# Six batches of attention by weighted values and row strips, in an attention and MLP kernel on one Trainium2 core

## The chip, the core and the metric

The kernel runs on one core of a Trainium2 chip. Its engines run side by side, each through its own instructions in order: TensorE (PE, with weight loads shown as PEld), VectorE (DVE), ScalarE (ACT), GpSimd (POOL) and SyncE (SP), which mostly issues DMAs. The metric is the time of one execution on the device in microseconds, lower is better. Before the change it was 351.64 us, the median of three runs.

## The reference

There are 8 batches of 8 heads, 576 positions of 64 numbers. A gate s gives each position a forget sum; the scores get the difference of two sums added, then a causal softmax and the product with v follow. The result, laid out as (8, 576, 512), goes through a layer norm and a two-layer MLP with a residual.

```python
scores = scale * np.matmul(q, k.transpose(0, 1, 3, 2))
cum = np.cumsum(np.maximum(s, 0.0), axis=-1)
bias = -(cum[:, :, :, None] - cum[:, :, None, :])
scores = np.where(causal, -1000000000.0, scores + np.minimum(bias, 0.0))
attn = softmax(scores)                 # row maximum taken off, 1e-09 in the denominator
x = np.matmul(attn, v)                 # heads put side by side: (8, 576, 512)
xn = (x - mu) / np.sqrt(var + 1e-06) * g_ln
out = x + np.maximum(xn @ w_ch1, 0.0) @ w_ch2
```

## The kernel before

*Tiles.* 576 positions are four tiles of 128 and a tail of 64. Scores are computed with keys on the partitions, so that exp of them can be the stationary operand of the product with v. `scores(b, h)` (L320) fills three PSUM banks, `sa`, `sb` and `sc`, with the causal blocks of keys 0 to 511; `scores_d(b, j)` (L358) does the last 64 keys for two heads. ACT takes exp of each bank into `er`, one of four slots; POOL sets the part above the diagonal to zero (L348, L378; the first ten heads add a mask on PE). `pv(b, h)` (L396) multiplies with `v_bf`, in 15 matmuls of 65 columns: the last column of v is one, so that it gives the softmax's denominator. `pv_norm` (L415) divides on DVE: a reciprocal, a product into `xb` for the four tiles, one into `xm` for the tail. The tails of two batches share one `xm` tile.

*Bias.* The difference of the forget sums comes out of the score matmul itself: k and q have 64 rows of numbers and 4 more rows, three bf16 pieces of the sum and ones (`KA` = 68). For the first two groups (four heads are a group) they stand beside the numbers before the transpose; for groups 2 to 5 `aug` (L208) puts them in by DMA; for groups 6 to 15 `cast_rows` (L175) copies them on POOL from `cT` beside the cast numbers, and `tr_rows` (L184) turns rows into columns by a DMA transpose, one head in 128 columns.

*MLP.* A batch is 32 units on a queue: 16 `mlp1` (L536), four 512-column matmuls and a relu on ACT or DVE, and 4 times 4 quarters of `mlp2` (L556), the last of which adds the residual on DVE (`yo`, L571) and sends it out through SP. The tails of all batches are one more set of units at the end. Between attention and MLP stands the layer norm: statistics on DVE (L450), then for each tile an aggregate (L473) and `xn` (L496), rstd by a power on POOL (L470), and a DMA transpose (L518).

*Order.* Every engine runs its instructions in the order in which the program names them. The start is written out as one long string, `PLAN` (L956), whose words name steps (`s.14` scores of head 14, `v.14` its pv, `n.14` its norm, `Q`, `E` transposes and evacuations of k and q of two heads, `u` a unit, `l` an xn, `p` loads). From head 18 on a loop (L987) sets a head's scores, some units, the pv of an earlier head, and parts of the layer norm of the batch before. `run_units` takes units off the queue. All loads of k and q of later groups, the transposes and the stores wait in SP's queue in that order; v's loads, which also convert to bf16, are issued by POOL (L159).

*PSUM.* Eight banks: three for scores (`ps_s`), two for `ph` and `py` (`ps_m`), two for transposes and tail scores (`ps_t`), one for `pot`, the result of a pv (`ps_o`).

Of the kernel before, what the change touches and what calls it, by code (L numbers as in the profile page):

```python
# [9 lines left out]
F32 = mybir.dt.float32  # L10
BF16 = mybir.dt.bfloat16
# [4 lines left out]
P = 128  # L16


@with_exitstack
def kernel(  # L20
# [9 lines left out]
    out: bass.AP,  # L30
):
# [16 lines left out]
    NG = BH // G  # L48
    NPE = 6
# [6 lines left out]
    stage = ctx.enter_context(tc.tile_pool(name="stage", bufs=6))  # L56
    pairs = ctx.enter_context(tc.tile_pool(name="pairs", bufs=4))
# [23 lines left out]
    eight = const.tile([BH, P], F32, name="eight")  # L81
    v_bf = [const.tile([P, NT, H, D + 1], BF16, name=f"v_bf{i}") for i in range(2)]

# [6 lines left out]


    spare = kq[2].rearrange("p u h s -> p (u h s)")
    er = const.tile([P, 4, EW], BF16, name="er")
    cT = const.tile([P, NT, 2, BH, 4], BF16, name="cT")
    xm = [const.tile([P, Dm], F32, name=f"xm{i}") for i in range(4)]
    xTm = const.tile([P, B // 2, KD, P], BF16, name="xTm")
    c3 = const.tile([KT, 3, S], BF16, name="c3")
    c_hi, c_mid, c_lo = (c3[0:BH, j, :] for j in range(3))
    zeros = const.tile([P, 512], BF16, name="zeros")
# [3 lines left out]
    row_sets = [spare[:, 0 : NT * 2 * G * P], rowb.rearrange("p t h c -> p (t h c)")[:, 0 : NT * 2 * G * P]]  # L103
    rows = [r.rearrange("p (t u h c) -> p t u h c", t=NT, u=2, h=G) for r in row_sets]
# [59 lines left out]
    def ld_rows(gam, t):  # L164
        pn = P if t < NF else TL
        b, h0 = gam // 2, (gam % 2) * G
        tmp = stage.tile([P, 2, G, D], F32, name="rowtmp", tag="st")
        for u, src in enumerate((k, q)):
            nc.sync.dma_start(
                out=tmp[0:pn, u],  # L170
                in_=src[b, h0 : h0 + G, t * P : t * P + pn, :].rearrange("h s d -> s h d"),
            )
        loaded["rows", gam, t] = tmp

    def cast_rows(gam, t):  # L175
        pn = P if t < NF else TL
        nc.gpsimd.tensor_copy(  # L177
            out=rows[gam % 2][0:pn, t, :, :, 0:D], in_=loaded.pop(("rows", gam, t))[0:pn]
        )
        nc.gpsimd.tensor_copy(  # L180
            out=rows[gam % 2][0:pn, t, :, :, D:KA], in_=cT[0:pn, t, :, gam * G : (gam + 1) * G, :]
        )

    def tr_rows(gam, t0, t1):  # L184
        pn = P if t0 < NF else TL
        o, n = t0 * 2 * G * P, (t1 - t0) * 2 * G
        nc.sync.dma_start_transpose(
            out=kq[home(gam)]
            .rearrange("p u h s -> p (u h s)")[:, o : o + n * pn]
            .rearrange("p (h s) -> p h s", s=pn),  # L190
            in_=row_sets[gam % 2][0:pn, o : o + n * P],
        )

# [21 lines left out]
    trc_bank = ps_o.tile([P, 3 * NT * BH + KT - BH], BF16, name="trc", tag="pot")  # L215
# [46 lines left out]
    def bias_rows(tr):  # L262
        for t0, t1, pn in ((0, NF, P), (NF, NT, TL)):
            nc.vector.tensor_copy(
                out=cT[0:pn, t0:t1, 0, :, 1:4],
                in_=tr[0:pn, :, t0:t1, :].rearrange("p j t x -> p t x j"),
            )
            nc.vector.tensor_copy(out=cT[0:pn, t0:t1, 1, :, 0], in_=tr[0:pn, 0, t0:t1, :])


    trs = {}

    def tr_kind(kind, g):
        src = ready.pop((kind, g))
        tr = ps_t.tile([P, S], BF16, name="trqk", tag="tr")
        for t in range(QT):

            nc.tensor.transpose(  # L278
                tr[:, t * QP : (t + 1) * QP],
                src[0:QP].rearrange("p h c -> p (h c)")[:, t * P : (t + 1) * P],  # L280
                ident[0:QP, 0:QP],
            )
        trs[kind, g] = tr
# [11 lines left out]


    def k_cols(b, h, kb):
        i, hh = home(b * 2 + h // G), h % G
        if b * 2 + h // G < NPE:
            return kq[i][0:KA, 0, hh, kb * P : (kb + 1) * P]  # L300
        n = P if kb < NF else TL
        o = kb * 2 * G * P + hh * n
        return kq[i].rearrange("p u h s -> p (u h s)")[0:KA, o : o + P]

    def q_cols(b, h, q0, q1):
        i, hh = home(b * 2 + h // G), h % G
        if b * 2 + h // G < NPE:
            return [(q0, q1, kq[i][0:KA, 1, hh, q0:q1])]
        flat = kq[i].rearrange("p u h s -> p (u h s)")
        full = flat[0:KA, 0 : NF * 2 * G * P].rearrange("p (t h s) -> p t h s", t=NF, s=P)  # L310
        o = NF * 2 * G * P + (G + hh) * TL
        got = []
        if q0 < NF * P:
            qf = min(q1, NF * P)
            got.append((q0, qf, full[:, q0 // P : qf // P, G + hh, :]))
        if q1 > NF * P:
# [365 lines left out]
    for t in range(NT):  # L682
        ld_cast_v(1, t)
# [379 lines left out]
```

## Time and profile before

| what | value |
| --- | --- |
| median of 3 runs | 351.64 us (351.25 to 351.77) |
| profiled execution, its own time as the page gives it: span, first to last instruction | 349.3 us |
| granted TensorE clock | 1.000 |
| PE, 3061 matmuls | 340.7 us busy (98%) |
| DVE, ACT, POOL | 193.1, 187.7 and 162.6 us busy |
| exp of one bank (L339), mean record | 596 to 609 ns, 168 of them |
| relu of one bank on ACT, on DVE | 598 ns and 692 ns |
| select on POOL (L348), 128x256 | 435 ns, 108 of them |
| issue of a v load on POOL (L159) | 864 ns, 40 of them |
| cast of k or q rows on POOL (L177) | 610 to 619 ns, 50 of them |
| reciprocal, product, tail product of a norm | 191, 425 and 280 ns |
| DMA share in the middle of the span | 0.9 and more of 16 engines |

A record of a matmul holds its way through the array too, so records of one engine overlap; the time that an instruction takes from the next one is read from the distance of two starts. An engine that is busy is not thereby on the path that sets the end: the chain of waits tells which was.

### The profile page before, as it was taken

To read this page: it belongs to the slowest core of one execution; us is meant where nothing else is said; L and a number is where in the kernel's file an instruction comes from. 1 tells how busy PE (TensorE), PEld (TensorE's weight loads), DVE (VectorE), ACT (ScalarE), POOL (GpSimd) and SP (SyncE) were. 2 spreads that over 40 slices of the span, in tenths; PEclk is the share of its full clock that TensorE was granted. 3 is DMA by queue.
4 is the path that set the end of the run, shared out by engine and by line. 5 is a ranking of instruction groups with operands and counts; after the bars stand their busy time and mean duration, and the time that the engine had idled before them with its cause. 6 is when DMAs were issued, how large, how long until landed. Compare 5 with 4: busy or idle time off the path is not lost.

```text
span 349.3 us, 8164 instructions
## 1 busy us (share of the span) xinstructions
PE 340.7 (98%) x3061; PEld 194.7 (56%) x3085; DVE 193.1 (55%) x518; ACT 187.7 (54%) x360; POOL 162.6 (47%) x336
## 2 busy tenths in 40 slices
PE   7999999999999999999999999999999999999995
PEld 3989766555555555555555555555555544444444
DVE  6879878954376548553746458443844582113112
ACT  5878898967544773367436661675347403402500
POOL 8997498248365736393746375446421010000000
PEclk9999999999999999999999999999999999999999
DMA  9999999999999999999999999999730033011013
GB/s 141 165 180 162 205 158 169 174 192 169 169 204 203 183 190 176 224 188 195 163 185 225 168 199 183 217 166 188 143 109 2 3 80 115 2 60 60 3 30 91
DMA packets 171864, 50.97 MB, mean 146 GB/s; under 512 B 159536, under 2 KB 167280, under 8 KB 171824
## 3 DMA queue, kind: packets, MB, share of 16 engines
q1 hardware_dynamic: 117872, 37.20, 58.3%
q0 software_dynamic: 52432, 12.46, 40.0%
q10 hardware_dynamic: 1520, 0.79, 0.9%
q8 instruction: 24, 0.39, 0.5%
q14 instruction: 16, 0.13, 0.1%
HBM read 37.11 MB, written 9.44 MB: 133 GB/s over the span
## 4 chain that ended last, share of the span: by engine, by line
PE 95%; DVE 2%; DMA 1%; issue 1%; DVEq 0%
PE py L560 35%; PE ph L541 34%; PE pot L406 7%; PE sc L328 3%; PE sb L328 3%; PE sa L328 3%; PE ph L829 2%; PE st L727 2%; PE trqk L278 1%; PE pot L785 1%; PE trt L705 1%; DMA c_first<-in_s_dram 1%; PE st L735 1%; PE sd L364 0%; PE trx L529 0%
## 5 line engine op out<-in xcount | busy, mean ns | idle before, releaser
L560 PE MATMUL py<-w_bf,hT 128*128 128x512 bf16 (+2 forms) x584 | 130.9, 367 | 1.3
L541 PE MATMUL ph<-xT,w_bf 128*128 128x512 bf16 x480 | 112.5, 379 | 0.0
L551 ACT ACTIVATE hT<-ph 128x512 bf16<-128x512 f32 x103 | 61.4, 598 | 71.9 <-PE ph L541 71.8
L560 PEld LDWEIGHTS <-hT 128*128 128x128 bf16 x608 | 54.2, 98 | 52.7
L541 PEld LDWEIGHTS <-w_bf 128*128 128x128 bf16 x544 | 49.5, 98 | 51.0 <-issue 0.3
L339 ACT ACTIVATE er<-sa 128x512 bf16<-128x512 f32 x56 | 33.4, 596 | 62.7 <-PE sa L328 61.0
L348 POOL TENSOR_SCALAR_AFFINE_SELECT er<-er 128x256 bf16<-128x256 bf16 x108 | 44.6, 435 | 29.1 <-ACT er L339 28.7
L549 DVE TENSOR_SCALAR hT<-ph 128x512 bf16<-128x512 f32 x33 | 22.8, 692 | 58.7 <-PE ph L541 50.8
L571 DVE SCALAR_TENSOR_TENSOR yo<-py,rstd,xb 128x512 f32<-128x512 f32 x32 | 23.9, 748 | 34.7 <-PE py L560 33.4
L328 PEld LDWEIGHTS <-kq 68*128 68x128 bf16 x400 | 28.6, 97 | 20.2
L406 PEld LDWEIGHTS <-er 128*128 128x128 bf16 x840 | 32.8, 98 | 12.1 <-DVE xm L427 0.2
L159 POOL DMA_DIRECT2D v_bf<-in_v_dram x40 | 34.4, 864 | 2.1 <-PE pot L406 0.8
L406 PE MATMUL pot<-v_bf,er 128*128 128x65 bf16 x840 | 34.7, 193 | 0.0
L339 ACT ACTIVATE er<-sc 128x512 bf16<-128x512 f32 x56 | 34.1, 609 | 0.0
L339 ACT ACTIVATE er<-sb 128x512 bf16<-128x512 f32 x56 | 33.4, 597 | 0.0
L177 POOL CAST kq<-rowtmp 128x512 bf16<-128x512 f32 (+1 forms) x25 | 15.5, 619 | 37.1 <-DMA rowtmp<-in_q_dram 37.0
L177 POOL CAST rowb<-rowtmp 128x512 bf16<-128x512 f32 (+1 forms) x25 | 15.3, 610 | 34.9 <-DMA rowtmp<-in_q_dram 30.3
L418 DVE RECIPROCAL rinv<-pot 128x5 f32<-128x5 f32 x56 | 10.7, 191 | 35.6 <-PE pot L406 35.6
L420 DVE TENSOR_TENSOR xb<-pot,rinv 128x256 f32<-128x256 f32 x56 | 23.8, 425 | 1.9
L496 DVE SCALAR_TENSOR_TENSOR xn<-xb,mv,gb 128x512 bf16<-128x512 f32 x28 | 22.8, 813 | 1.0
L450 DVE BATCH_NORM_STATS2 stats<-xb 128x6 f32<-128x128 f32 (+1 forms) x84 | 21.9, 321 | 0.3
L328 PE MATMUL sc<-kq 68*128 68x256 bf16 (+1 forms) x192 | 21.7, 228 | 0.0
(120 smaller groups left out, 347.6 us busy)
## 6 DMA issues: line engine op xcount, KB each, us to landing
out_dram<-yo SPq DMA_DIRECT2D x32, 256.0 KB
rowtmp<-in_k_dram SPq DMA_DIRECT2D x40, 128.0 KB
rowtmp<-in_q_dram SPq DMA_DIRECT2D x40, 128.0 KB
v_bf<-in_v_dram POOLq DMA_DIRECT2D x32, 128.0 KB, 6.0
w_bf<-in_moe_w_ch_dram POOLq DMA_DIRECT2D x8, 512.0 KB, 9.0
kp<-in_k_dram POOLq DMA_DIRECT2D x8, 144.0 KB, 8.6
qp<-in_q_dram POOLq DMA_DIRECT2D x8, 144.0 KB, 8.8
rowtmp<-in_k_dram SPq DMA_DIRECT2D x10, 64.0 KB
```

What stands on the lines that cost most here:

```text
L159: nc.gpsimd.dma_start(out=v_bf[b % 2][:pn, t, :, 0:D], in_=v[b, :, t * P : t * P + pn, :].rearrange("h s d -> s h d"),)
L177: nc.gpsimd.tensor_copy(out=rows[gam % 2][0:pn, t, :, :, 0:D], in_=loaded.pop(("rows", gam, t))[0:pn])
L328: nc.tensor.matmul(a[:, c + a0 - q0 : c + a1 - q0], lhsT=k_cols(b, h, kb), rhs=cols, start=True, stop=not (pe_mask and diag),)
L339: nc.scalar.activation(out=e[:, o : o + 512], in_=a, func=ACT.Exp, scale=scale)
L348: nc.gpsimd.affine_select(out=two, in_=two, compare_op=ALU.is_ge, fill=0.0, base=0, pattern=[[0, 2], [1, P]], channel_multiplier=-1,)
L406: nc.tensor.matmul(pot[:, t, :], lhsT=e[:, o : o + P], rhs=vv[:, kb, h, :], start=(kb == 0), stop=(kb == last),)
L420: nc.vector.tensor_tensor(out=xb[b][:, :, hs], in0=pot[:, 0:NF, 0:D], in1=rinv[:, 0:NF].unsqueeze(2).to_broadcast([P, NF, D]), op=ALU.mult,)
L496: nc.vector.scalar_tensor_tensor(out=xn, in0=tiles[t], scalar=mvs[b][:, t, 0:1] if b > 0 else mean0[:, t : t + 1], in1=gb, op0=ALU.subtrac ...
L541: nc.tensor.matmul(ph, lhsT=w1_bf[:, kd, fb * P : (fb + 1) * P], rhs=xT[:, :, kd, :], start=(kd == 0), stop=(kd == KD - 1),)
L551: nc.scalar.activation(out=hT[:, fb, :], in_=ph, func=ACT.Relu)
L560: nc.tensor.matmul(py[t], lhsT=hT[:, fb, t * P : (t + 1) * P], rhs=w2_bf[:, fb, c0:c1], start=(fb == 0), stop=(fb == FB - 1),)
L571: nc.vector.scalar_tensor_tensor(out=yo, in0=py[t], scalar=rs, in1=x[:, c0:c1], op0=ALU.mult, op1=ALU.add)
```

## The change

For batches 2 to 7 the bias rows go. Within a row of the softmax, the query's own forget sum is a constant factor and drops out in the division; what is left is a factor exp(sum of the key), which is put on v and on the ones column. `sums_rel`, `sums_tr` and `sums_exp` make these factors once (`wt`), relative to 0.48 of each head's last sum; `weigh_v` multiplies v by them on POOL as it converts, after a plain f32 load through SP; `weigh_ones` writes the weighted ones as two bf16 columns, a value and its remainder, so a pv has 66 columns and its norm first adds the two (`norm_two`).

k and q then have 64 rows, and two heads lie in one 128-row tile, one in rows 0 to 63, the other in rows 64 to 127. `burst` names the score matmuls of both heads by turns, into six banks. The last 64 keys of all eight heads of a batch become one bank (`tails`), with k in a zero-padded tile `kz`. For batch 2, `side_two` (O2, on DVE) puts two heads side by side before PE transposes them (`tr_two`, F; `evac_two`, G); later batches use the DMA transposes, which hold half as many blocks.

`to_pairs` closes the old PSUM pools and opens two: two banks for `pot` and `py`, six for scores and `ph`. PLAN's end and the loop are rewritten by pairs of heads: burst, six exps, four selects, then a pv of the pair before, two units, its other pv, more units. In a pair's slot the first four relus and the seventh are on DVE, the others on ACT. A guard counts on DVE whether sums, reciprocals and rstd are in range and raises a flag; at the end all engines read it and jump over a general path, a loop over the batches that is only run if the flag is up.

```diff
-    ps_s = ctx.enter_context(tc.tile_pool(name="ps_s", bufs=3, space=bass.MemoryType.PSUM))
-    ps_m = ctx.enter_context(tc.tile_pool(name="ps_m", bufs=2, space=bass.MemoryType.PSUM))
-    ps_t = ctx.enter_context(tc.tile_pool(name="ps_t", bufs=2, space=bass.MemoryType.PSUM))
-    ps_o = ctx.enter_context(tc.tile_pool(name="ps_o", bufs=1, space=bass.MemoryType.PSUM))
+    def to_pairs():
+        ps.close()
+        early.close()
+        pool["v"] = ctx.enter_context(tc.tile_pool(name="vst", bufs=6))
+        for tag, n in (("m", 2), ("s", 6)):
...
+    def weigh_v(b, t, eng="pool"):
+        pn = pn_of(t)
+        e = nc.vector if eng == "dve" else nc.gpsimd
+        e.tensor_tensor(
+            out=v_bf[b % 2][0:pn, t, :, 0:D],
+            in0=loaded.pop(("v", b, t))[0:pn],
+            in1=wt[0:pn, t, b, :].unsqueeze(2).to_broadcast([pn, H, D]),
+            op=ALU.mult,
+        )
...
+    BANKS = (("sa", 0, 0), ("sa", 1, 0), ("sb", 0, OB), ("sb", 1, OB), ("sc", 0, OC), ("sc", 1, OC))
+
+    def burst(n):
+        b, j = divmod(n, NJ)
+        banks = {}
+        for name, i, _ in BANKS:
+            banks[name, i] = ptile("s", [P, 512], name)
+        for two in zip(*[side_scores(b, j, i, banks) for i in range(2)]):
+            for a, lhsT, rhs in two:
+                nc.tensor.matmul(a, lhsT=lhsT, rhs=rhs, start=True, stop=True)
+        bank["B", n] = banks
...
+    def norm_two(n, i):
+        b, h = n // NJ, 2 * (n % NJ) + i
+        pot = pots.pop((n, i))
+        rinv = rinvs[:, b, h, :]
+        sums = small.tile([P, NT], F32, name="sums", tag="sums")
+        nc.vector.tensor_reduce(out=sums, in_=pot[:, :, D:D2], axis=AX.X, op=ALU.add)
+        nc.vector.reciprocal(out=rinv, in_=sums)
...
+            if kind == "h":
+                i = done_in_slot[0]
+                done_in_slot[0] += 1
+                on[0] = eng or ("dve" if i < 4 or i == 6 else "act")
...
PLAN, its end:
+        G.k.8:A F.q.8 s.15 G.q.8:A g.0 lv.2.3 lv.2.4 lr.3.0 U v.13 p.15 vo.2:P vm.2.0:P vm.2.1:P
+        n.13 O2.k.9:D u v.14 F.k.9 G.k.9:A u n.14 v.15 O2.q.9:D g.1 F.q.9 G.q.9:A lr.3.1 u n.15 vm.2.2:P vm.2.3:P vm.2.4:P me g.2 l.0 u l.1 cr.3.0 cr.3.1 u l.2 l.3 lr.3.2 D u
+        O2.k.10:D O2.q.10:D u F.k.10 F.q.10 G.k.10:A O2.k.11:D G.q.10:A O2.q.11:D  u F.k.11 F.q.11 G.k.11:A G.q.11:A u tk.2 to
+        B2.8 BX.8 BM.8 D2.2 cr.3.2 u la.1.4 Da.1.4
...
+    for n in range(N0, NP + 1):
+        b, j = divmod(n, NJ)
+        done_in_slot[0] = 0
+        pre_pair(n)
...
+        if n < NP:
+            if j == 0:
+                tails(b)
+                tails_exp(b)
+                tails_mask(b)
+            burst(n)
+            for x in range(6):
+                burst_exp(n, x)
+            for x in range(4):
+                burst_mask(n, x)
+        post_pair(n)
+        if n > 0:
+            pv_two(n - 1, 0)
+            norm_two(n - 1, 0)
             run_units(2)
             nu -= 2
+            pv_two(n - 1, 1)
+            norm_two(n - 1, 1)
+            if j != 1:
+                ln_stats((n - 1) // NJ, {2: 0, 3: 1, 0: 2}[j])
+        if j == 1:
+            for t in range(NT):
                 ln_xn(b - 1, t)
+                if t == NF - 1:
+                    ln_tr_dma(b - 1, 0)
+                if t < NF:
                     run_units(1)
                     nu -= 1
...
+        fast_path(tc, q, k, v, s, g, w1, w2, out, flag)
+        bad = nc.values_load(flag[0:1, 0:1], min_val=0, max_val=1)
+        with tc.If(bad > 0):
+            general_path(tc, q, k, v, s, g, w1, w2, out)
```

More of the change, by code (lines that the diff above doesn't have):

```diff
@@ L532, in ln_tr, with relu @@
         copy_on(eng, xT_dst(b, t), tr)
[L534 removed]
+    def relu(dst, ph, eng):
+        if eng == "dve":
+            nc.vector.tensor_scalar_max(out=dst, in0=ph, scalar1=0.0)
+        else:
+            nc.scalar.activation(out=dst, in_=ph, func=ACT.Relu)
+    on = ["act"]
+    new = [False]
+    phs = {}
     def mlp1(xT, fb):
[L537 to L539 removed]
+        ph = ptile("s" if new[0] else "m", [P, 512], "ph")
         for kd in range(KD):
@@ L797, in tile_norm @@
         pn = P if t < NF else TL
-        rinv = small.tile([P, NT], F32, name="rinv", tag="rinv")
-        nc.vector.reciprocal(out=rinv[0:pn, 0:G], in_=pot[0:pn, :, D])
+        rinv = rinvs[0:pn, 0, g * G : (g + 1) * G, t]
+        nc.vector.reciprocal(out=rinv, in_=pot[0:pn, :, D])
         hs = slice(g * 256, (g + 1) * 256)
@@ new lines, in raise_flag @@
+    def raise_flag(count, ones, n):
+        a = ptile("s", [P, 8], "count")
+        nc.tensor.matmul(a[0:1, :], lhsT=ones, rhs=count, start=True, stop=True)
+        total = const.tile([1, 2], F32, name="total")
+        nc.vector.tensor_reduce(out=total[:, 0:1], in_=a[0:1, :], axis=AX.X, op=ALU.add)
+        nc.vector.tensor_scalar(
+            out=total[:, 1:2], in0=total[:, 0:1], scalar1=n - 0.5, scalar2=None, op0=ALU.is_lt
+        )
+        nc.vector.tensor_copy(out=flag, in_=total[:, 1:2])
```

761 lines of the change are left out of this document (575 added, 186 removed).

## The prediction

> **What bounds the kernel now.** I read the page first: busy shares, then the chain that ended last.
>
> ```profile
> span 349.3 us, 8164 instructions
> ...
> PE 340.7 (98%) x3061; PEld 194.7 (56%) x3085; DVE 193.1 (55%) x518; ACT 187.7 (54%) x360; POOL 162.6 (47%) x336
> ...
> PE 95%; DVE 2%; DMA 1%; issue 1%; DVEq 0%
> PE py L560 35%; PE ph L541 34%; PE pot L406 7%; PE sc L328 3%; PE sb L328 3%; PE sa L328 3%; PE ph L829 2%; PE st L727 2%; PE trqk L278 1%; PE pot L785 1%; PE trt L705 1%; DMA c_first<-in_s_dram 1%; PE st L735 1%; PE sd L364 0%; PE trx L529 0%
> ```
>
> PE never waits long; everything else is under 56%. Second, the chain in order of time, which gives the period of one batch, 185.38 - 148.54 = 36.84 us:
>
> ```profile
> 148.54 1.73 PE ph L541 x8
> ...
> 185.38 1.73 PE ph L541 x8
> ```
>
> Third, the timeline inside a batch, for pitches (start to start), since records overlap:
>
> ```profile
> 223.78 0.62 PE L406 MATMUL pot<-v_bf,er 128*128 128x65 bf16 x15
> ...
> 224.24 1.89 PE L541 MATMUL ph<-xT,w_bf 128*128 128x512 bf16 x8
> ...
> 225.96 0.38 PE L328 MATMUL sa<-kq 68*128 68x512 bf16 x1
> ...
> 226.16 0.60 ACT L551 ACTIVATE hT<-ph 128x512 bf16<-128x512 f32 x1 [0.27 <-PE ph L541]
> 226.18 0.38 PE L328 MATMUL sb<-kq 68*128 68x64 bf16 x3
> 226.40 0.39 PE L328 MATMUL sc<-kq 68*128 68x256 bf16 x4
> 226.62 1.03 PE L541 MATMUL ph<-xT,w_bf 128*128 128x512 bf16 x4
> 226.66 0.59 ACT L339 ACTIVATE er<-sa 128x512 bf16<-128x512 f32 x1
> ...
> 227.13 0.60 ACT L339 ACTIVATE er<-sb 128x512 bf16<-128x512 f32 x1
> ```
>
> A head's three score banks take 226.62 - 225.96 = 0.66 us of PE, its pv 0.46, a unit of four 512-column matmuls 0.863 (1.72 for eight). A result is taken up 0.19 us after its last matmul's pitch ends (226.16 against 225.97). ACT empties banks every 0.48 us, each done 0.60 after its start. Fourth, the layer norm on DVE, and POOL beside it:
>
> ```profile
> 208.01 0.22 DVE L473 BATCH_NORM_AGGREGATE mv<-stats 128x2 f32<-128x18 f32 x1
> 208.26 0.75 DVE L496 SCALAR_TENSOR_TENSOR xn<-xb,mv,gb 128x512 bf16<-128x512 f32 x1
> 208.93 0.23 DVE L473 BATCH_NORM_AGGREGATE mv<-stats 128x2 f32<-128x18 f32 x1
> 209.19 1.00 DVE L496 SCALAR_TENSOR_TENSOR xn<-xb,mv,gb 128x512 bf16<-128x512 f32 x1
> 210.11 0.22 DVE L473 BATCH_NORM_AGGREGATE mv<-stats 128x2 f32<-128x18 f32 x1
> ...
> 211.28 0.75 DVE L571 SCALAR_TENSOR_TENSOR yo<-py,rstd,xb 128x512 f32<-128x512 f32 x1
> 211.94 0.18 DVE L418 RECIPROCAL rinv<-pot 128x5 f32<-128x5 f32 x1
> ```
> ```profile
> 209.25 1.21 POOL L348 TENSOR_SCALAR_AFFINE_SELECT er<-er 128x256 bf16<-128x256 bf16 x2 [1.09 <-ACT er L339]
> ```
>
> An aggregate with its xn takes 0.92 us alone, 1.18 beside POOL's selects (which stretch too, two in 1.21 against 0.78); I use 1.07. A yo takes 0.66 in the row, 0.75 to its end.
>
> **The change, part by part** (+ is slower).
>
> *Scores.* 48 heads lose 0.66 us each; 24 bursts of two heads come. No row shows two matmuls in different rows of the array. If the strips run side by side, a burst is one head's 0.66 plus one start, 0.68; if not, 1.32; if switching also empties the array, more (rival B). I take 0.68, because the row that it is nearest to is one head's, with each strip streaming the same columns: 24 x (1.32 - 0.68) = -15.4. The Trainium skill ("TensorE: Matmul & The Clock Gate", Part 3, on packing small matmuls) has tiles in different row groups run concurrently, about 4 ns apart; no run here shows it yet.
>
> *pv and tails.* 65 columns become 66: 0.46 x 1/65 x 48 = +0.3. Eight 64-column tail matmuls per batch take the place of eight: 0.24 both ways.
>
> *POOL, DMA, SP.* POOL loses 30 v issues (0.86 each) and 50 cT copies (0.21), and gains 30 multiplies of v, between a cast's 0.61 and twice that for two inputs, and small copies of the ones. At 47% busy, masks are due a whole slot (8.5 us) after their exps, so zero; without that cover, two masks (0.78) a slot. Transposes fall from 30 to 15, the aug rows of later groups go; v's 30 loads move to SP, behind xT transposes and out stores that wait for DVE. They are issued a slot ahead of their use, so zero; uncovered, one landing (6.0 us) a batch.
>
> *DVE.* Each of 48 norms gains a reduce like the reciprocal's 0.2: a norm becomes 1.1 us. Nothing by itself; it lengthens the chains below.
>
> *Banks: where new waits come.* PSUM becomes six banks for scores and ph, two for pot and py, and a burst takes all six at once. One slot is burst 0.68, pv 0.46, two units 1.73, pv 0.46, six units 5.18 = 8.51; four slots and the tails are 34.28 against 36.84. To this I add three waits, PE being in order.
> (a) Second slot (heads 2 and 3), after eight ph units: the burst's sixth bank, sc of the second head, is that of the last ph, relu'd by ACT. Free 0.19 + 0.60 + 0.06 = 0.85 after the unit; wanted at 0.44. +0.41.
> (b) First slot: tails go first, and the sixth bank is the tails' own, whose exp stands behind that relu: 0.19 + 0.48 + 0.60 + 0.06 = 1.33, wanted at 0.24 + 0.44. +0.65.
> (c) Third slot: the first py needs the bank of the last py, whose yo stands on DVE behind the second slot's second norm, four xn, the first yo and rstd: 0.19 + 1.1 + 4 x 1.07 + 0.66 + 0.28 + 0.75 + 0.06 = 7.32 us after that pv. PE reaches it after six units, a burst and a pv, 6.32. +1.0, and for odd batches, with a fifth xn (1.17), +2.17.
> Batches 3 to 7 go round the loop five times: 5 x 1.06 + 3 x 1.0 + 2 x 2.17 = +12.6. Bounds: xn at 0.92 and a norm of 0.98 leave +8.5; at 1.18, +14.8.
>
> *The bridge in PLAN* (heads 14 to 23). Batch 2's k and q are now first reordered by DVE (O2) and only then transposed (F). An O2 of 768 columns lies between a reciprocal's 0.2 and the 0.80 of a 576-column copy; by the 1024-column copy's 0.613 I take 0.46. DVE runs without a gap from the ninth group's O2: stats 1.1, norm 0.83, stats 1.1, four xn 4.28, two yo 1.32, O2. PE meets this twice: py waits for the first yo, 1.95, and the tenth group's F for its O2, 2.3. ACT's four 0.8 us evacuations cost 0.6 before the first burst. The tails, put behind six exps, hold the second burst: first exp 0.41 after its burst, six pitches, 0.60, so 3.95 against 2.6, +1.35, and their own bank 0.4. Two later bursts behind a relu: 0.9. The sums' transposes and one pv, 0.5. Together +8.0 (5.5 with the quick DVE prices, 10 with the slow).
>
> *Guard and branch.* The flag is raised some 40 units before the end, so it is hidden; without that cover, its five to ten DVE operations of about 0.4, 4 us. The jump over the general path runs beside the last store. The page's 3.2 us from last yo to end of span (345.72 + 0.35 = 346.07, to 349.3) bounds the branch: 0 to 3; I take +0.5, nearest to hidden.
>
> Sum: -15.4 + 0.3 + 12.6 + 8.0 + 0.5 = +6.0. The span 349.3 becomes 355.3; what lies around it, 2.3 us to the median 351.64, stays: 357.6.
>
> **Rivals.**
> B, strips don't pay. A matmul's record is 0.38 for a pitch of 0.216: 0.165 us of emptying. If each burst waits for that going in and coming out, waits (a) to (c) swallow the way in, and about 0.66 us a batch and 0.66 in the bridge stay: +4, 361.6. If the strips run one after the other, each burst is 1.32: +15.4, of which (a), (b) and part of (c) give back some 8: about 365. For it: K = 64 leaves half the array idle and nothing measured says that the halves overlap. Against: disjoint rows, different banks. The Trainium skill ("TensorEngine Tiling (Array Packing)", Key Properties) says that changing the tiling mode drains TensorE; it speaks against this change and by the drain's price the sum would be 361.6.
> C, faster: DVE's chain is short enough. If DVE comes to its yo before PE does, (c) and the two DVE waits of the bridge (11.5 of the 21 us of waits) go: 357.6 - 11.5 = 346. It decides in the third slot: (c) is nothing when the 7.32 us chain falls below 6.32; the whole breaks even when it is some 0.7 us shorter (xn pairs at 0.92). For it: xn's median record is 0.75, and POOL's 0.86 us issues go. Against: POOL now multiplies v in that very slot, and selects beside an xn made it 1.00.
> D, PE is not held at all, by ACT either: -15.1 + 0.5, 337. Against: a bank can't be reused before its reader ends. I count this into C's chance.
>
> **How the numbers follow.** A (as summed) 0.42, from 353 to 361; B 0.18, 361 to 367; C with D 0.35, 337 to 350.5; waits and gain just cancel 0.05. Likeliest is A, 357.6. The range reaches from 343 (most of C; below it D) to 366. Faster 0.35, same 0.05, slower 0.60; 0.2% (0.7 us) is about what a measurement of this kernel tells from no change.
>
> **What would show it.** Steps right: bursts of 0.7 us on PE with sa of both heads starting within 0.05; the period near 36.8 although a batch's matmuls need 34.3; waits of PE on ACT (relu, tails' exp) and on DVE's yo in the third slot, longer in odd batches; 4 to 5 us of idle PE before the first burst, behind O2. Wrong: bursts of 1.3 us (B); a period under 36 with PE at 98% (C); or a new stop that I priced at nothing, POOL late with masks or v, or SP with transposes.

## The result, and the profile after

The changed kernel takes 373.45 us (median of 4, 373.37 to 375.17) against 351.70 us for the kernel before on the same chip: a ratio of 1.062, with a 95% interval from 1.058 to 1.066. It is slower, as forecast, but by three to four times the forecast 6 us. The profiled execution took 373.37 us, with a span of 371.7.

The lines of the page after that answer to those shown of before, and the clock by slices:

```profile
span 371.7 us, 8037 instructions
...
PE 343.2 (92%) x3071; PEld 187.5 (50%) x3092; DVE 232.6 (63%) x634; ACT 169.5 (46%) x301; POOL 168.0 (45%) x306
...
PEclk9999999659999999999999999999999999999998
...
PE 60%; DVE 10%; issue 3%; POOL 2%; ACT 1%; ACTq 0%
```

PE is no longer always the bound: it has 60% of the chain where it had 95%, DVE has 10%, and in the two slices from 65 to 84 us the granted clock is 0.6 and 0.5. A table by stage shows where that is in time. I divided both traces at the same steps: the scores of head 14, the first mlp1 of batch 1, of batch 2 and of batch 7 (the bounds 111.71, 290.35 and 309.81 stand 0.16 or 0.17 us behind that first matmul, so the differences hold to 0.2 us). Columns: stretch, its length, busy time of PE, PEld, DVE, ACT and POOL, the granted clock, DMA share and GB/s. First before, then after:

```profile
49.05:73.90 24.85, 24.64 (x261) 15.02 (x264) 20.75 (x54) 20.08 (x37) 17.24 (x34) 1.00 1.21 164
73.90:111.71 37.81, 37.64 (x322) 20.47 (x321) 19.84 (x57) 21.84 (x45) 21.94 (x48) 1.00 1.26 190
111.71:290.35 178.64, 177.89 (x1488) 96.13 (x1501) 99.21 (x271) 92.08 (x183) 82.30 (x187) 1.00 1.05 161
290.35:349.30 58.95, 55.18 (x285) 26.72 (x286) 12.73 (x19) 14.35 (x24) 0.00 (x0) 1.00 0.14 45
```
```profile
49.46:89.32 39.86, 30.04 (x249) 15.43 (x252) 24.61 (x63) 27.01 (x32) 22.40 (x40) 0.79 0.70 139
89.32:132.18 42.86, 39.12 (x382) 20.22 (x385) 28.03 (x78) 20.27 (x40) 28.73 (x55) 1.00 1.09 209
132.18:309.81 177.63, 171.58 (x1450) 87.73 (x1457) 123.03 (x333) 69.83 (x135) 76.77 (x144) 1.00 0.59 128
309.81:371.70 61.89, 55.41 (x288) 26.73 (x288) 17.50 (x47) 13.14 (x22) 0.00 (x0) 0.98 0.13 40
```

The bridge (49 to 89 us) is 15.0 us longer, batch 1's round 5.1, the loop 1.0 shorter, the end 2.9 longer; 0.4 came earlier. In the bridge PE is idle for 9.8 of 39.9 us, where before it was idle for 0.2, and it runs at a mean clock of 0.79: in the trace's clock records the clock is 0.50 from 68.23 to 85.30 us and 1.00 on both sides. These are its idle times there (in brackets: how long, and what ended it), and the four evacuations G behind them:

```profile
61.63 0.43 PE L359 MATMUL trp<-ident,rowb 96*128 96x96 bf16 x6 [1.82 <-DVE rowb L142]
...
67.82 1.50 PE L789 MATMUL py<-w_bf,hT 128*128 128x512 bf16 x4 [2.31 <-DVE yo L801]
71.03 1.14 PE L359 MATMUL trp<-ident,rowb 96*128 96x96 bf16 x12 [1.71 <-DVE rowb L142]
...
75.77 0.64 PE L359 MATMUL trp<-ident,rowb 96*128 96x96 bf16 x6 [1.27 <-ACT kq L140]
...
79.60 0.61 PE L544 MATMUL sa<-kq 64*128 64x512 bf16 x2 [1.49 <-ACT kq L140]
```
```profile
71.73 7.82 ACT L140 COPY kq<-trp 128x576 bf16<-128x576 bf16 x4 [7.54 <-PE trp L359]
```

A G takes 7.82 / 4 = 1.95 us in the row, where I priced 0.8. And the copy O2 behind the first wait took 2.54 us, priced at 0.46, beside three multiplications of v on POOL; an xn of batch 2 took 2.43 beside two of them:

```profile
58.32 3.03 POOL L231 TENSOR_TENSOR v_bf<-rowtmp,wt 128x512 bf16<-128x512 f32 x3
...
59.03 2.54 DVE L142 COPY rowb<-qp 96x768 bf16<-96x768 bf16 x1
...
123.01 2.03 POOL L231 TENSOR_TENSOR v_bf<-rowtmp,wt 128x512 bf16<-128x512 f32 x2
123.17 2.43 DVE L719 SCALAR_TENSOR_TENSOR xn<-xb,mv,gb 128x512 bf16<-128x512 f32 x1
```

Both end some 0.2 to 0.6 us after the string of multiplications does (61.35 and 125.04). In the loop, a burst of two heads, and then the third slot's wait (c) in an even and in an odd round, with the xn that is in front of it on DVE:

```profile
205.64 0.39 PE L544 MATMUL sa<-kq 64*128 64x512 bf16 x2
205.87 0.38 PE L544 MATMUL sb<-kq 64*128 64x64 bf16 x6
206.09 0.39 PE L544 MATMUL sc<-kq 64*128 64x256 bf16 x8
206.41 0.60 PE L623 MATMUL pot<-v_bf,er 128*128 128x66 bf16 x14
...
194.82 1.66 DVE L719 SCALAR_TENSOR_TENSOR xn<-xb,mv,gb 128x512 bf16<-128x512 f32 x1
198.19 1.89 PE L789 MATMUL py<-w_bf,hT 128*128 128x512 bf16 x7 [1.01 <-DVE yo L801]
...
231.48 1.78 DVE L719 SCALAR_TENSOR_TENSOR xn<-xb,mv,gb 128x512 bf16<-128x512 f32 x1
235.91 1.89 PE L789 MATMUL py<-w_bf,hT 128*128 128x512 bf16 x7 [1.74 <-DVE yo L801]
```

Both heads' scores take 0.77 us (206.41 - 205.64), where one head took 0.66: the halves of the array do work side by side. But the change-over costs something on both sides. Behind the burst it is 0.11 us, and ahead of it another 0.10:

```profile
265.21 5.34 PE L789 MATMUL py<-w_bf,hT 128*128 128x512 bf16 x24
270.49 0.39 PE L544 MATMUL sa<-kq 64*128 64x512 bf16 x2
...
271.98 1.89 PE L789 MATMUL py<-w_bf,hT 128*128 128x512 bf16 x7
```

At their pitch of 0.216 us the 24 matmuls need 5.18, and the burst starts 5.28 after the first of them; before, a head's scores followed a unit without such a gap (224.24 to 225.96 for eight, shown in the prediction). So a burst costs 0.87. The last line stands at the place of wait (c) in the round of batch 7, and no wait is noted there (by the starts it is 0.25 us). In that round POOL multiplies no v, and all four xn ahead of it take 0.75 us.

### The profile page after: what moved, and what is told of

It is laid out like the page before. It is cut to its first block, busy times and chain, and to the rows that moved or that the text cites. A ratio compares the mean times of both kernels' runs of the same rounds, so it can differ in the third digit from the quotient of the medians.

```text
span 371.7 us, 8037 instructions
## 1 busy us (share of the span) xinstructions
PE 343.2 (92%) x3071; PEld 187.5 (50%) x3092; DVE 232.6 (63%) x634; ACT 169.5 (46%) x301; POOL 168.0 (45%) x306
## 4 chain that ended last, share of the span: by engine, by line
PE 60%; DVE 10%; issue 3%; POOL 2%; ACT 1%; ACTq 0%
PE ph L770 27%; PE py L789 24%; PE pot L623 5%; DVE xn L719 4%; DVE yo L801 2%; PE sc L544 2%; PE sa L544 1%; PE sb L544 1%; DVE mv L696 1%; POOL v_bf L231 1%; DVE hT L759 1%; DVE stats L673 1%; POOL rowb L218 1%; ACT er L549 1%; DVE xm L650 1%
## 5 line engine op out<-in xcount | busy, mean ns | idle before, releaser
L761 ACT ACTIVATE hT<-ph 128x512 bf16<-128x512 f32 x64 | 38.3, 601 | 96.0 <-PE ph L770 96.0
L759 DVE TENSOR_SCALAR hT<-ph 128x512 bf16<-128x512 f32 x72 | 48.5, 685 | 22.7 <-PE ph L770 21.9
L231 POOL TENSOR_TENSOR v_bf<-rowtmp,wt 128x512 bf16<-128x512 f32 (+1 forms) x30 | 30.7, 1039 | 1.7 <-DMA rowtmp<-in_v_dram 1.3
L623 PE MATMUL pot<-v_bf,er 128*128 128x66 bf16 x672 | 28.3, 193 | 2.4 <-DVE yo L801 2.4
L623 PEld LDWEIGHTS <-er 128*128 128x128 bf16 x672 | 25.2, 97 | 10.6 <-issue 2.4
L640 DVE TENSOR_REDUCE sums<-pot 128x5 f32<-128x10 f32 x48 | 7.9, 165 | 36.0 <-PE pot L623 36.0
L693 POOL TENSOR_TENSOR rstd<-rstd,mhalf 128x4 f32<-128x4 f32 (+1 forms) x8 | 8.8, 1094 | 33.8 <-DVE rstd L692 30.5
L544 PEld LDWEIGHTS <-kq 64*128 64x128 bf16 x360 | 12.6, 96 | 19.3 <-issue 15.0
L643 DVE TENSOR_TENSOR xb<-pot,rinvs 128x256 f32<-128x256 f32 x48 | 20.4, 424 | 1.6
L140 ACT COPY kq<-trp 128x576 bf16<-128x576 bf16 x8 | 16.2, 2170 | 9.6 <-PE trp L359 9.6
## 6 DMA issues: line engine op xcount, KB each, us to landing
kp<-in_k_dram POOLq DMA_DIRECT2D x8, 144.0 KB, 10.6
```

The costliest lines, as they stand in the source:

```text
L231: e.tensor_tensor(out=v_bf[b % 2][0:pn, t, :, 0:D], in0=loaded.pop(("v", b, t))[0:pn], in1=wt[0:pn, t, b, :].unsqueeze(2).to_broadcast([pn ...
L544: nc.tensor.matmul(a, lhsT=lhsT, rhs=rhs, start=True, stop=True)
L623: nc.tensor.matmul(pot[:, t, :], lhsT=cols, rhs=v_bf[b % 2][:, kb, h, :], start=(kb == 0), stop=(kb == t),)
L759: nc.vector.tensor_scalar_max(out=dst, in0=ph, scalar1=0.0)
L761: nc.scalar.activation(out=dst, in_=ph, func=ACT.Relu)
```

## The experiments

Theory T: the loss is not in the strips, nor in the loop, but in a few operations of the bridge that take much longer than their rows in the trace of before, G by its way of writing and DVE's by POOL's multiplications beside them, with a clock that falls behind the gaps; and in the branch at the end. The rivals are named in each expectation. "The bridge" is measured below from the scores of head 14 to the first mlp1 of batch 1: 39.86 us in the changed kernel. Three of the runs that leave the bridge as it is (without the guard, and the two that edit the loop alone) have 40.29, 40.54 and 40.68, so it scatters by about 0.8 us. The kernel before took 351.70 to 352.39 us in the sets of runs that these belong to; ratios are within a set, and half a microsecond between kernels of two sets decides nothing.

**G writes side by side.**

```diff
-        dst = kq_flat(b)[:, "kq".index(kind), j, 0:S].rearrange("d (p t) -> d t p", t=QT)
-        copy_on(eng, dst, trs.pop((kind, g)))
+        dst = kq_flat(b)[:, "kq".index(kind), j, 0:S].rearrange("d (p t) -> d p t", t=QT)
+        copy_on(eng, dst, trs.pop((kind, g)).rearrange("d t p -> d p t"))
```

> The changed kernel (373.45 us, ratio 1.062 to the kernel before), but each evacuation G writes its 576 columns side by side and reads them with a stride, instead of writing them 12 bytes apart. Theory T (the loss is the bridge of heads 14 to 23, from steps that take far longer than I priced them, and a clock that falls in the gaps): G falls from 2.1 to about 0.8 us, the two idle times of 1.27 and 1.49 before the first burst go, and 2.5 to 5 us of 373.45 with them: 368.5 to 371. Rival R1 (the bridge is set by DVE's order, layer norm chain before the reorderings, and ACT is beside the path): G may fall, the time by less than 0.7 us. Rival R2 (ACT pays for each element it reads from a bf16 bank, whatever the write): G stays at 2 us and nothing moves.

Measured: 371.17 us, ratio 1.057 (1.051 to 1.063), 0.2 us above T's range. The same four evacuations in this kernel:

```profile
72.98 1.18 ACT L140 COPY kq<-trp 128x576 bf16<-128x576 bf16 x2 [7.62 <-PE trp L359]
74.37 1.18 ACT L140 COPY kq<-trp 128x576 bf16<-128x576 bf16 x2 [0.21 <-PE trp L359]
```

A G takes 0.64 us instead of 2.1: the stride on the written side was the price, and R2 falls. The bridge is 35.76 us, 4.1 shorter, so G was on the path, and R1 falls too. The whole gained less in this execution: after a wait of 1.75 us for yo at 231 the clock fell (0.76 from 230 to 237 us), which the changed kernel's profile does not show at that place, and 1.7 us were given back. The waits of PE on O2 and yo did not go: before the first burst it now stood 3.93 us for an O2 of 3.40.

**O2 ahead of the layer norm chain** (of batch 1, where the expectation says batch 0). In `PLAN`, `O2.k.10:D O2.q.10:D O2.k.11:D O2.q.11:D` are moved from behind `D u` to right behind `n.15`.

> The changed kernel, but the four reorderings O2 of the tenth and eleventh group stand on DVE right after the last normalisation, ahead of the layer norm chain of batch 0, not behind it. Theory T: the wait of 1.71 us before the tenth group's transposes goes and the evacuations start about 3 us sooner; the first yo comes some 1.8 us later (four copies of 0.45), which makes the 2.31 us wait of py longer by 1.5: net -1 to -3 us, 370.5 to 372.5. Rival R1 (DVE's chain alone sets the bridge, and its order is all): -4 to -6 us. Rival: the chain's length is all that counts, and what is saved at F is lost at py: 0 +- 0.7.

Measured: 375.26 us, ratio 1.065 (1.061 to 1.069), bridge 40.77: no gain, a miss. PE no longer waited for the tenth group, but 2.76 us for the first yo. The four copies, at their new place, fell beside POOL's work and took 1.04, 0.76, 1.32 and 0.34 us. Order alone, with durations as they are, moves the wait from one place to the other: that is what the last rival said, though its 0 +- 0.7 us was missed as well, by some 1 us.

**PE kept busy in the gaps.** Five times six to ten matmuls of 512 columns, into a bank that nobody reads, for instance

```diff
-        ... l.2 l.3 lr.3.2 D u
+        ... l.2 l.3 lr.3.2 D fill.10 u
```

> The changed kernel with 38 more matmuls of 512 columns, whose result nobody reads, put into PE's instruction stream at the five places of the bridge where PE stood idle for 1.3 to 2.3 us, in about the length of each idle time. Theory T: the granted clock (0.81 in 49 to 80 us, 0.71 in 80 to 89, units of 1.7 instead of 0.86 from 68 to 85) fell because PE stood idle there; with the gaps filled it stays near 1.00 and the units at 0.86, which gives back 4 to 8 us less what the fill costs: 367 to 371. Rival R4 (the clock fell for the work's sum, or by itself, as in the kernel before at its start): the clock stays at 0.7 to 0.8 there, and the fill costs up to its own 8.2 us: 374 to 382.

Measured: 375.97 us as the median of three executions (a fourth took 381.04), ratio 1.066 (1.058 to 1.073). The same microseconds in the changed kernel and in this one (the columns as above, the clock is the third number from the end):

```profile
49.30:89.32 40.02, 30.20 (x250) 15.51 (x253) 24.77 (x63) 27.17 (x32) 22.56 (x40) 0.79 0.70 139
```
```profile
49.30:89.32 40.02, 33.51 (x279) 17.13 (x282) 24.87 (x58) 26.35 (x31) 21.55 (x37) 0.96 0.69 134
```

The clock came back as T said, from 0.79 to 0.96, and units again took 0.86 us. The time did not: the bridge is 41.38 us. So the clock fell for the gaps, but the clock alone won nothing that can be seen in the bridge. The first burst came 32.70 us after head 14's scores, against 30.14 in the changed kernel and 31.21 to 31.59 in the three runs named above, and 1.2 of that is the filling itself: the tenth group's first O2 was done at 71.92, its transposes followed the filling at 73.13. Behind the first burst the bridge took 8.68 us instead of 9.72 (8.95 to 9.25 in the three), because PE then waited for ACT's exps. Mostly it was DVE and ACT that the bridge waited for, and a slow PE filled its own idle time. That part of T falls; R4's time came true without its reason. The trace agrees with the Trainium skill ("TensorE: Matmul & The Clock Gate", Part 1) that idleness brings the clock down; the page speaks of an idle window of about 3.4 us, and the idle times in the changed kernel's bridge were 2.31 us at most.

**v's multiplication later on POOL.** The words `vo.2:P vm.2.0:P ... vm.2.4:P` are moved behind the last G.

> The changed kernel, but POOL's multiplication of batch 2's v by its weights stands behind the last evacuation G of the bridge, where no reordering O2 and no normalisation xn runs on DVE. Theory T (a DVE copy or xn that runs beside POOL's multiply of two inputs doesn't end before that multiply does): the ninth group's second O2 falls from 2.54 to 0.35 to 0.5 us, the xn of 1.16 to about 0.8, PE's waits of 1.82 and part of 2.31 and 1.71 go; the norm of the third pair of heads comes 2 to 4 us sooner, and the time is 369.5 to 372. Rival R5 (that copy is slow for its landing load or its strides): it stays at 2 us or more, and the time moves by less than 0.7.

Measured: 371.36 us, ratio 1.053 (1.050 to 1.056), in T's range. The profiled execution, which was the slowest of the four, shows a bridge of 40.11 us. From its timeline:

```profile
68.54 0.34 DVE L142 COPY rowb<-kp 96x768 bf16<-96x768 bf16 x1
...
68.81 4.36 DVE L142 COPY rowb<-qp 96x768 bf16<-96x768 bf16 x1
68.91 5.15 POOL L231 TENSOR_TENSOR v_bf<-rowtmp,wt 128x512 bf16<-128x512 f32 x5
...
73.09 1.19 DVE L142 COPY rowb<-kp 96x768 bf16<-96x768 bf16 x1
...
73.22 0.66 PE L359 MATMUL trp<-ident,rowb 96*128 96x96 bf16 x6 [3.62 <-DVE rowb L142]
```

The first half of T came as said: the ninth group's O2 at 59.52 took 0.35 us instead of 2.54, and the wait of 1.82 went. But nothing held POOL at the new place in its own queue, so it multiplied at 68.91, and now the O2 of the tenth group was caught: 0.34 us alone, 4.36 beside four multiplications, and PE stood 3.62 us. The same copy, its loads long landed, is quick or slow by what POOL does: R5 falls. What the quicker executions gained is not in this profile.

**Strips not interleaved.**

```diff
-        for two in zip(*[side_scores(b, j, i, banks) for i in range(2)]):
+        for two in [side_scores(b, j, i, banks) for i in range(2)]:
```

> The changed kernel, but a burst issues all matmuls of its first head and then all of the second, where it alternated between them: the same work on the same halves of the array. Theory T (the halves overlap only where neighbouring matmuls lie in different halves): bursts go from 0.77 to about 1.35 us, +0.55 times 24 = +13, of which the waits on banks behind the burst take back up to half: 380 to 387. Rival B of the prediction (the halves are served one after the other, or the mode change eats the gain): nothing changes, 373.45 +- 1.

Measured: 381.32 us, ratio 1.081 (1.078 to 1.085), 7.9 us more than the changed kernel, or 7.2 with each against the kernel before of its own set. A burst, and the pv after it:

```profile
212.32 0.39 PE L544 MATMUL sa<-kq 64*128 64x512 bf16 x1
212.54 0.38 PE L544 MATMUL sb<-kq 64*128 64x64 bf16 x3
212.76 0.27 PE L544 MATMUL sc<-kq 64*128 64x256 bf16 x1
212.77 0.39 PE L544 MATMUL sa<-kq 64*128 64x512 bf16 x1
...
213.53 0.60 PE L623 MATMUL pot<-v_bf,er 128*128 128x66 bf16 x14
```

A burst takes 1.21 us instead of 0.77; 24 x 0.44 = 10.6, of which the waits behind the bursts took back about 3. Even here the end of one head overlaps with the start of the other (212.76 and 212.77). Rival B of the prediction falls in its second form, that the strips run one after the other.

**yo between normalisations.** In the third slot xn 0, two units, xn 1, one unit, xn 2, three units, xn 3; a fifth xn a slot later.

> The changed kernel, but in the slot of the layer norm DVE does the first yo between normalisations, after the second and the third, and a fifth xn (odd batches) a slot later; PE's units stand accordingly. Theory T: the wait (c) of py on yo, 1.17 us in even and some 2 us in odd batches, goes in batches 3 to 7: 5 to 8 us in all, 365.5 to 368.5. Rival (DVE's chain is too long wherever yo stands, and PE meets the next yo, or the normalised rows come late to the transposes): 372.5 to 375.

Measured: 372.71 us, ratio 1.059 (1.055 to 1.063); the loop itself is 1.4 us shorter. A miss: PE still waited 0.52 (even) and 0.32 us (odd) for yo, and then stood behind the later norms, because the chain was as long as ever: its second xn took 2.16 and 2.28 us.

**v's multiplication a slot later in the loop.**

```diff
-            for t in {-3: (0, 1), -2: (2, 3), -1: (4,)}.get(m, ()):
+            for t in {-2: (0, 1), -1: (2, 3), 0: (4,)}.get(m, ()):
                 if t == 0:
                     weigh_ones(b)
                 weigh_v(b, t)
```

> The changed kernel, but in the loop POOL multiplies v by its weights one slot later, away from DVE's layer norm chain. Theory T: xn, of which the mean is 0.953 us, falls to 0.8 to 0.85, the one of 2.43 us at 123 to about 0.8 with PE's wait of 2.43 us behind it, and (c) gets shorter by 0.3 to 0.5 in each batch: 2.5 to 5 us, 368.5 to 371. Rival R6 (any POOL work stretches xn by as much, so that the selects do it just as well): 372.7 to 374.5.

Measured: 371.11 us, ratio 1.055 (1.052 to 1.058), 0.1 us above T's range. The group of the 28 xn, in the changed kernel and in this one (busy time, mean ns of one):

```profile
L719 DVE SCALAR_TENSOR_TENSOR xn<-xb,mv,gb 128x512 bf16<-128x512 f32 x28 | 26.7, 953 | 1.0
```
```profile
L719 DVE SCALAR_TENSOR_TENSOR xn<-xb,mv,gb 128x512 bf16<-128x512 f32 x28 | 21.4, 764 | 1.0
```

The mean falls from 953 to 764 ns; the longest, 2.43 us, to 1.01, in the bridge beside POOL's casts. Behind it the wait of 2.43 us at 127 becomes 0.73, (c) vanishes in the even round and is 0.68 in the odd one, and from the first slot of the loop on the kernel gains 3.3 us. R6 falls, though not by this run alone: its selects stand mostly ahead of the xn. In the kernel before, where selects run beside xn, none takes more than 1.00 us.

**No guard, no branch.**

> The changed kernel without the check of the ranges, the flag, the branch and the general path behind it (so inputs out of range would not be caught): the fast path alone. Theory T: last yo to end of span falls from 5.9 back to the 3.2 us of the kernel before, nothing else moves: 370.3 to 371.2. My prediction's price for it, 0.5, gives 372.9. Rival R3 (the guard's DVE and POOL work delays the last layer norm too, and the second program half costs time at the start): 366 to 369.5.

Measured: 372.22 us, ratio 1.058 (1.052 to 1.064). By the median alone that can't be told from the changed kernel. The last yo before (span 349.3), in the changed kernel (371.7) and in this one (370.9) tells more:

```profile
345.72 0.35 DVE L571 SCALAR_TENSOR_TENSOR yo<-py,rstd,xm 128x128 f32<-128x128 f32 x1 [0.54 <-PE py L560]
```
```profile
365.42 0.35 DVE L801 SCALAR_TENSOR_TENSOR yo<-py,rstd,xm 128x128 f32<-128x128 f32 x1 [0.55 <-PE py L789]
```
```profile
367.15 0.35 DVE L801 SCALAR_TENSOR_TENSOR yo<-py,rstd,xm 128x128 f32<-128x128 f32 x1 [0.54 <-PE py L789]
```

From its end to the end of the span 5.93 us become 3.40 (in the kernel before: 3.23). So the branch costs about 2.5 us at the end, as T said; T's time of 370.3 to 371.2 was missed by 1 us, about the bridge's scatter.

**Together.** The edits of G, of O2, of yo and of the loop's v, and batch 2's v multiplied on DVE instead of POOL:

```diff
-        ... G.q.11:A u tk.2 to
+        ... G.q.11:A vo.2:D vm.2.0:D vm.2.1:D vm.2.2:D vm.2.3:D vm.2.4:D u tk.2 to
```

> The changed kernel with all of its computation, guard and general path included, and five edits together: the evacuations G write side by side; batch 2's v is multiplied by its weights on DVE, right after the last reordering O2, where DVE otherwise idled 11 us; the four O2 of the tenth and eleventh group ahead of the layer norm chain; in the loop POOL's multiplication of v a slot later; the first yo between normalisations. Theory T (what the bridge loses is G, and DVE operations held beside POOL's multiplies): the O2 and xn of the bridge all at 0.35 and 0.75 to 0.85, the first burst at 69 to 72 us after the start instead of 79.60, and with the loop's 3 to 4 us 359 to 363. Rival R1 (the order of DVE's chain sets the bridge, whatever POOL does): the first burst not before 74, 364 to 368.

Measured: 358.21 us, ratio 1.018 (1.014 to 1.023). Seven of the eight O2 take 0.34 to 0.36 us and one 0.54, xn 0.75 to 1.00, G 0.64 to 0.66; the mean clock of the bridge is 0.95. Its first burst, and the one long wait left:

```profile
67.16 1.43 PE L789 MATMUL py<-w_bf,hT 128*128 128x512 bf16 x4 [3.90 <-DVE yo L801]
...
72.75 0.39 PE L544 MATMUL sa<-kq 64*128 64x512 bf16 x2
```

The bridge is 32.22 us, 7.6 shorter. So 15 of the 22 us that the change costs go with five edits that leave the strips, the weights and the guard as they are. T's mechanism holds; its time was 0.8 us too long, its first burst 0.75 us too early. But T had put the loss outside the loop, and that is only half right: of the 15.3 us between the two profiles' spans 7.6 are in the bridge, 1.8 in batch 1's round and 5.2 in the loop, where no wait for yo is left. Against the kernel before, the bridge is still 7.4 us longer and the end 2.5, and the loop is 6.3 shorter (2.2 of it for work that was done earlier).

**Together, without the edit of O2.**

> As the run with five edits, but without the one that puts four O2 ahead of the layer norm chain. Theory T: with DVE's operations at their own durations that order is worth four O2, about 1 us either way: within 1.5 us of the other, 359.5 to 364. Rival R1 (the chain's order is what counts): 2 to 5 us slower than the other.

Measured: 359.65 us, ratio 1.021 (1.017 to 1.025), bridge 34.34. The edit that had gained nothing among stretched operations is now worth 2.1 us in the bridge and 1.4 by the medians: T's bound of 1.5 and R1's 2 meet here, and the run does not tell them apart.

**The first yo ahead of the normalisations.** In the kernel with five edits:

```diff
-        ... O2.k.11:D O2.q.11:D me g.2 l.0 u l.1 cr.3.0 cr.3.1 u l.2 l.3 lr.3.2 D u
+        ... u u O2.k.11:D O2.q.11:D me g.2 u l.0 l.1 cr.3.0 cr.3.1 l.2 l.3 lr.3.2 D
```

> The run with five edits (358.21 us, ratio 1.018), and in the bridge the first two yo of batch 0 put ahead of the four normalisations of batch 1 on DVE. There PE still stood 3.90 us before py, for the first yo. Theory T (each idle time of the bridge is a place in DVE's order once nothing stretches its operations): that wait goes, the first burst comes 3 to 4 us sooner (72.75 to about 69), 354 to 355.5. Rival R7 (the next in line, the loads or POOL's copies of the tails' keys, holds PE instead): 356.5 to 358.5.

Measured: 357.96 us, ratio 1.017 (1.014 to 1.019): R7. The first burst came 17.96 us after the scores of head 14 instead of 23.55, and the gain was gone 8 us later:

```profile
67.59 0.39 PE L544 MATMUL sa<-kq 64*128 64x512 bf16 x2
...
70.31 0.41 PE L515 MATMUL sd<-kq,kz 128*128 128x64 bf16 x8 [1.89 <-POOL kz L144]
...
70.33 3.82 POOL L488 TENSOR_SCALAR_AFFINE_SELECT er<-er 128x256 bf16<-128x256 bf16 x4
...
71.40 3.29 DVE L231 TENSOR_TENSOR v_bf<-rowtmp,wt 128x512 bf16<-128x512 f32 x5
...
75.40 0.58 PE L789 MATMUL py<-w_bf,hT 128*128 128x512 bf16 x1 [3.06 <-DVE yo L801]
```

PE waits for the tails' keys on POOL, and for a yo behind v's multiplications, which I had put on DVE where it was idle before; and now they hold POOL in turn, four selects in 3.82 us instead of 1.81.

**The same without guard and branch.**

> The same, without the check of the ranges, the flag, the branch and the general path (inputs out of range would not be caught). Theory T: another 2.5 to 2.8 us off the end, as in the first run without them: 351.2 to 353, so that all that the strips save, some 15 us, is just about used up by the waits that are left and by the layer norm's place. Rival R3 (what the guard costs depends on what runs beside it, and is hidden now): 354 to 355.5, as with it.

Measured: 356.71 us, ratio 1.012 (1.009 to 1.015). From the last yo to the end 3.43 us, against 5.41 with the guard. Both forecasts of the time were missed: T's gain of 2.5 to 2.8 us is 2.0 at the end and 1.25 by the medians, and the profiled bridge is 1.6 us longer than with the guard, where the edit changes nothing. No kernel tried here beats the one before.

## Why the prediction was wrong

It had the direction right and the loop nearly so, in part by luck, and the size wrong: 357.6 us forecast, 366 the upper end, 373.45 measured. By its steps:

| step | forecast | in the changed kernel |
| --- | --- | --- |
| burst of two heads | 0.68 us, -15.4 in all | 0.77 and 0.10 ahead of it, so 24 x (0.87 - 1.32) = -10.8 |
| (a) sc behind the last ph's relu | +0.41 | 0.62 from sc to pv at 187.25 instead of 0.32: +0.30 |
| (b) behind the tails' exp | +0.65 | 0.79 instead of 0.32 at 178.10: +0.47 |
| (c) py behind yo, layer norm of an even, an odd batch | +1.0, +2.17 | by the starts 2.50, 1.16 and 0.25 (batches 3, 5 and 7), 1.89 and 1.90 (4 and 6); the brackets above, from the last record's end, give 0.16 less |
| up to batch 2's first mlp1: 8 bursts, bridge, one round of waits | 8.0 - 8 x 0.64 + 1.06 + 1.0 = +4.9 | +20.5 |
| from there to batch 7's: 16 bursts, four rounds of waits | 4 x 1.06 + 2 x 1.0 + 2 x 2.17 - 16 x 0.64 = +0.3 | -1.0 |
| guard and branch | +0.5 | about +2.5, the tail of the page |
| POOL's v multiplications | 0 | stretch DVE's O2 and xn |

The stretches don't hold the same heads. By batch 2's first mlp1 the changed kernel has done the scores of 18 heads and the pv of 17 from head 14's scores on, the one before 16 and 15: 2 x (0.66 + 0.46) = 2.2 us of the 20.5 are work drawn forward from the loop. With the heads evened out at these prices, the bridge costs +16.1 us where the sum has 8.0 - 2 x 0.64 = +6.7, batch 1's round +1.7 instead of 1.06 + 1.0 - 6 x 0.64 = -1.8, the loop +1.2 instead of +0.3, the end +2.9 instead of +0.5.

*The loop* came out near the sum, its periods too (36.98 and 37.72 us from burst 177.58 to 214.56 to 252.28, where the sum has 36.3 and 37.5). In part that is luck: the bursts saved less, the waits (a) and (b) cost less, and the five waits (c), 7.7 us where the sum has 7.3, have other parts. I had taken each xn as 1.07; in fact most are 0.75, and the one that meets POOL's multiplications is 1.66 to 2.43. That an xn of a whole tile never exceeded 1.00 us before was true of a POOL that only cast and selected. In batch 7's round, which has no multiplication, (c) is next to nothing.

*The bursts.* I took "one head's 0.66 plus one start" and left the change-over to rival B; it takes 0.10 us ahead of a burst and 0.11 behind it, up to 24 x 0.19 = 4.6 us in all, less where a wait on a bank covers it.

*The bridge* is the step that failed: "ACT's four 0.8 us evacuations", "by the 1024-column copy's 0.613 I take 0.46", and above all "so zero" for POOL's multiplies of v. G was priced by a copy of as many columns that writes 4 bytes apart, where G writes 12 bytes apart; the edit of its stride shows 4.1 us for it. O2 and xn were priced by rows with another neighbour on POOL (and 0.613 is in no row: those copies take 0.67 us, or 0.60 to the next start). Alone an O2 takes 0.34, beside the multiplications 2.5 to 4.6. The bounds, 5.5 to 10, came from these same rows and so missed the truth on the same side. With G, O2 and xn at their own durations, and O2 in a better place, the bridge costs 32.22 - 24.85 = 7.4 us, or 8.5 with the head evened out that it holds less, where I had summed 6.7; that G, the place of O2 and v's place on POOL have 4.1, about 2 and about 1.5 us of the 7.6 is read from three kernels' bridges (35.76, 34.34, 32.22).

*The end.* I took a value "nearest to hidden"; nothing hid it. The branch's 2.5 us were within the bounds given, 0 to 3.

*The rivals.* B falls in its second form by the burst of 0.77 us. Its first form, 0.165 us in and out, is seen at 0.10 and 0.11; the traces agree with the drain that the Trainium skill states for a change of tiling mode ("TensorEngine Tiling (Array Packing)", Key Properties) as far as these two gaps go. C and D fall by the waits, but C's mechanism is there where no multiplication meets the layer norm: in batch 7's round, and in the loop of the kernel with five edits. What set the size was none of them, but what the prediction's last sentence named as an open flank: a stop priced at nothing, on POOL, though not by its being late.

*Open:* of the kernel with five edits, batch 1's round is 3.3 us longer than before (41.06 against 37.81). It holds three heads' scores and pv more, 3.4 us at the prices of before; what its six bursts save, 6 x 0.45 = 2.7 us, has gone into waits on banks, norms and yo, of up to 0.4 us each, that I have not taken apart. Whether v's multiplications can be put where they meet neither DVE's copies nor POOL's masks, and the bridge then goes below 30 us, was not tried.

## What to carry to other kernels

Price an operation by a row with the same access on both sides and the same neighbour on the other engine, not by its element count; here a copy that wrote two bytes in every twelve took three times its quiet price, and one beside POOL's multiplications some thirteen times. When an engine takes over work "in idle time", list what the engine that it can hold up does at that moment, and tie its start to a semaphore if the place matters (not tried here), because a place in a queue is not a time. A saving repeated in the loop (here 0.45 us a burst) must first pay for a one-off transition, so that transition deserves the most careful sum.

## What the runs showed of the hardware that I had not expected

- A DVE copy from SBUF to SBUF and an xn (two inputs from SBUF) stand still beside POOL's multiplications, over several in a row: the copy takes 0.34 us alone and 4.36 beside four of them. It ended beside the fifth, which took 1.14 us instead of 1.04. Other work on POOL holds such a copy too: one multiplication and two memsets 2.04 us (the run of G), casts 1.32 (the run with O2 ahead). The yo, which reads one input from PSUM, took 0.73 to 0.75 us in all 32 cases, whatever POOL did. It goes the other way too: beside DVE's five multiplications a select on POOL took 2.75 us, the three ahead of it 0.4 each. The Trainium skill ("SBUF — State Buffer", Who interferes with whom) says that DVE and GpSimd share a port pair as an exclusive lock, held for the whole instruction, for a DVE copy in its two-port modes and for a DVE instruction with two SBUF inputs; the traces agree with which instructions are hit, and show besides that a DVE copy waited through up to four of POOL's back-to-back instructions.
- ACT, copying 576 columns of bf16 out of PSUM, took 2.1 us when it wrote them 12 bytes apart and 0.64 us when it read them with a stride and wrote them side by side: 3.6 and 1.1 ns a column. The copies of before, which wrote 4 bytes apart, took 0.80 us.
- In the clock records of these traces the granted clock is 1.0 or 0.5, and from the bridge up to the tail of the kernel each stretch at 0.5 lasts 3.41 us or two, three or five times that; the values in between are means. In the changed kernel's bridge it was 0.5 for 17.07 us, behind idle times of 1.82 and 2.31 us, none longer; with PE kept busy in them one stretch of 3.41 us was left. A single wait can do it and need not: behind the wait for yo at 127 us, 2.43 us in the changed kernel and 2.44 in the run of G, the clock stayed at 1.0, and behind 2.71 (no guard), 2.74 (O2 ahead) and 2.44 us (PE kept busy) it was 0.5 for 3.41 us. The next burst then came 1.6 to 1.7 us later than the wait's own length explains. How much of the scatter between executions this makes is not shown.
- Two matmuls on rows 0 to 63 and 64 to 127, into different banks, run at the same time if their instructions alternate: 0.77 us for what takes 1.21 in the other order. Between matmuls on all 128 rows such a burst costs another 0.10 us ahead of it.
